# New instruction lengths for the planner of a two-problem sliding-window attention kernel

## The chip, the cores and the metric

The kernel runs on one core of a Trainium2 chip. The metric is device time in microseconds (us): medians of several executions, each with a 95% interval where two kernels are compared. All timed runs quoted here were fast, at a granted TensorE clock of 0.997 to 1.0.

## The reference

Two independent problems A and B of the same shape are computed and their outputs are put side by side:

```python
B, S, D = 1, 2048, 1024;  H = 32; Dh = 32; W = 256
qkv = (x @ wqkv)                        # 2048x1024 @ 1024x3072, bf16
scores = q @ k^T * Dh**-0.5             # causal, and only the last 256 keys
p = softmax(where(mask, scores, -1e9))
out = (p @ v) @ wo                      # 1024x1024
```

With blocks of 128 queries and 128 keys, the window leaves 45 blocks of scores per head instead of 256. Four heads are handled together (a "group"), so there are 16 groups, 8 per problem.

## The kernel before

The kernel runs in 180 **rounds**. A round computes the scores of four blocks for four heads into the one score buffer in PSUM (four times the size of a `pp` bank, see below), and ScalarE takes the exp of them in one instruction of 2048 columns. In 128 places between rounds TensorE adds up PV and the row sums (PV) of an earlier pair of query blocks. What is left of the round is filled with **projection chains**: eight 512-column steps (or sixteen of 256) that accumulate one output tile in one of two PSUM banks named `pp`. At its end a chain is copied to SBUF by a **cast**, on ScalarE or on VectorE, and the bank comes free.

A Python planner fixes this order when the program is built, with a small clock for each of three engines:

```python
NS_MM = 216.0
NS_ROW = 420.0        # scores of a round
NS_PV = 52.0          # one PV block of 128 columns
ACT_EXP = 1800.0
COST = {"act": 590.0, "dve": 670.0, "or": 560.0, "rinv": 930.0, "mult": 900.0,
        "edge": 620.0}

class _Clock:
    def chain(self):                      # a chain takes the bank that comes free next
        self.pe = max(self.pe, self.banks.pop(0))

    def evacuate(self, engines):          # who casts this chain?
        best = min(engines, key=lambda e: max(getattr(self, e), self.pe) + COST[e])
        end = max(getattr(self, best), self.pe + 150.0) + COST[best]
        setattr(self, best, end)
        self.banks.append(end)
        return best
```

`act` and `dve` are the times at which the planner believes ScalarE and VectorE to be done; `pe` is where TensorE is. The exp advances `act`, an edge add (`both`, the sum of two partly masked blocks that PV needs for its row sums) advances `dve` by `edge`. Norms come in two parts, a reciprocal (`rinv`) and two shuffles with a multiply (`mult`). These, and the ORs that gather a range check of q and k (`or`), first wait in a list called `side`:

```python
def run_side():
    cost, f, last = side.pop(0)
    f()                                   # puts the instruction into VectorE's queue
    clock.dve = max(clock.dve, clock.pe) + cost
    ...
def emit(now, budget):                    # after every projection step:
    ...
            if side and (clock.dve < clock.pe + 100.0 or len(side) > 8):
                run_side()
# in a round, after the scores:
        clock.act = max(clock.act, clock.pe) + ACT_EXP
        clock.exp = clock.act
# in the main loop: how many projection steps does the round get, and the end of the range check
    whole[0] = not (due and due[0][0] <= now)     # True: a round without PV
    ...
    emit(now, level(now) - fixed[now])            # fixed = NS_ROW + NS_PV * PV blocks
    if now >= sealed and len(certify) == 2:
        while side:
            run_side()                            # all that waits is flushed
        certify.pop(0)(top)                       # the check is read on VectorE
```

## Time and profile before

Time: 609.83 us median of 3 runs (609.81 to 610.95); with the runs beside the changed kernel, 609.85 us median of 6.

| | busy us | share |
|---|---|---|
| TensorE | 593.6 | 98% |
| VectorE | 468.4 | 77% |
| ScalarE | 441.1 | 73% |
| casts on ScalarE / VectorE | 191 / 66 | |
| rounds, first to last scores | 539.9 | |

### The profile page before, as it was taken

The page shows a single profiled execution, that of the slowest core. Times are in us where ns is not written, and L with a number is a line of the kernel's source. Part 1 is how long each engine was busy: PE and PEld are TensorE (multiplying, and loading weights), DVE is VectorE, ACT ScalarE, POOL GpSimd, SP SyncE. Part 2 cuts the span into 40 slices and gives each one's busy share as a digit, 9 for nine tenths or more (in the row PEclk, how much of TensorE's full clock was granted, in tenths as well). Part 3 has the DMA queues.
Part 4 walks back from the last instruction along what each step waited for, and adds up shares of the span by engine and source line. Part 5 has one row for each costly group of instructions (what it writes and reads, how often), then busy time and mean ns, then how long its engine had stood idle before and what let it go on. Part 6 is the DMA issues. An engine that isn't in the chain of part 4 may idle for free.

```text
span 607.6 us, 28768 instructions
## 1 busy us (share of the span) xinstructions
PE 593.6 (98%) x12786; PEld 344.3 (57%) x12838; DVE 468.4 (77%) x1199; ACT 441.1 (73%) x376; POOL 326.3 (54%) x630
## 2 busy tenths in 40 slices
PE   8999999999999999999999999999999999999996
PEld 6555466656655756564556756655455665545443
DVE  1677889898898898897888887898888887897200
ACT  3778887788888887877778877777776777785332
POOL 0565666665666666556555565555555655554000
PEclk9999999999999999999999999999999999999999
DMA  9833110111015501442111100112021040113222
GB/s 234 182 92 89 37 38 3 38 38 39 3 38 90 114 14 30 82 101 77 38 37 38 38 4 8 33 37 81 2 68 34 4 106 21 55 58 120 72 79 64
DMA packets 86802, 35.47 MB, mean 58 GB/s; under 512 B 65552, under 2 KB 86160, under 8 KB 86672
## 3 DMA queue, kind: packets, MB, share of 16 engines
q1 hardware_dynamic: 85632, 33.31, 22.2%
q8 instruction: 102, 1.67, 1.2%
q10 hardware_dynamic: 1040, 0.26, 0.2%
q14 instruction: 28, 0.23, 0.1%
HBM read 17.83 MB, written 8.39 MB: 43 GB/s over the span
## 4 chain that ended last, share of the span: by engine, by line
PE 96%; ACT 2%; issue 1%; DMA 1%; ACTq 0%
PE pp L176 44%; PE pp L172 28%; PE acc L513 13%; PE st L451 10%; ACT pt L459 1%; DMA oT<-in_A_x_dram 1%; PE acc L582 0%; PE pp L568 0%; ACT kT L190 0%; ACT vt L190 0%; PE st L582 0%; ACT osb L190 0%; PE pp L805 0%; ACTq L190 0%
## 5 line engine op out<-in xcount | busy, mean ns | idle before, releaser
L459 ACT ACTIVATE pt<-st 128x2048 bf16<-128x2048 f32 x180 | 338.0, 1878 | 91.6 <-PE st L451 73.5
L471 POOL TENSOR_SCALAR_AFFINE_SELECT pt<-pt 128x512 bf16<-128x512 bf16 x224 | 154.5, 690 | 145.7 <-ACT pt L459 143.1
L467 POOL TENSOR_SCALAR_AFFINE_SELECT pt<-pt 128x512 bf16<-128x512 bf16 x256 | 179.2, 701 | 85.8 <-ACT pt L459 85.8
L524 DVE RECIPROCAL rinv<-acc 128x128 f32<-128x128 f32 x128 | 122.0, 953 | 57.0 <-PE acc L513 56.4
L176 PE MATMUL pp<-xT,wqk 128*32 128x512 bf16 x2712 | 163.1, 379 | 0.0
L481 DVE TENSOR_TENSOR both<-pt 128x512 bf16<-128x512 bf16 x224 | 137.1, 651 | 0.0
L176 PEld LDWEIGHTS <-wqk 128*32 128x32 bf16 x2712 | 69.3, 97 | 54.2 <-issue 0.4
L172 PE MATMUL pp<-xT,wqk 128*128 128x512 bf16 (+1 forms) x323 | 76.7, 369 | 4.1 <-issue 2.4
L176 PE MATMUL pp<-wv,xT 128*32 128x256 bf16 x2436 | 75.9, 273 | 0.0
L451 PE MATMUL st<-qT,kT 32*128 32x384 bf16 (+2 forms) x1488 | 71.5, 269 | 0.1
L176 PEld LDWEIGHTS <-xT 128*32 128x32 bf16 x2436 | 63.8, 97 | 6.2
L529 DVE STREAM_SHUFFLE wide<-rinv 128x128 f32<-128x128 f32 x256 | 64.6, 298 | 0.0
L513 PE MATMUL acc<-pt,vt 128*32 128x128 bf16 (+1 forms) x2160 | 63.3, 239 | 0.0
L172 PE MATMUL pp<-wo_sb,oT 128*128 128x512 bf16 (+1 forms) x269 | 59.3, 373 | 1.3 <-issue 0.9
L451 PEld LDWEIGHTS <-kT 32*128 32x128 bf16 x1488 | 22.2, 92 | 64.5 <-issue 63.3
L190 ACT CAST osb<-pp 128x512 bf16<-128x512 f32 (+1 forms) x52 | 30.0, 577 | 39.1 <-PE pp L172 24.4
L531 DVE TENSOR_TENSOR oT<-acc,wide 128x256 bf16<-128x256 f32 x128 | 54.3, 425 | 4.4
L176 PE MATMUL pp<-wo_sb,oT 128*32 128x512 bf16 x952 | 55.6, 379 | 0.0
L172 PEld LDWEIGHTS <-wqk 128*128 128x128 bf16 x362 | 33.4, 98 | 37.0 <-issue 6.8
L172 PE MATMUL pp<-wv,xT 128*128 128x256 bf16 x415 | 50.9, 273 | 1.4 <-ACT kT L190 0.6
L513 PEld LDWEIGHTS <-vt 128*32 128x32 bf16 x2160 | 35.9, 96 | 26.4 <-issue 24.1
L172 PEld LDWEIGHTS <-xT 128*128 128x128 bf16 x415 | 38.9, 98 | 12.0 <-issue 6.1
(46 smaller groups left out, 386.5 us busy)
## 6 DMA issues: line engine op xcount, KB each, us to landing
out_dram<-osb SPq DMA_DIRECT2D x63, 128.0 KB, 1.8
wqk<-in_B_wqkv_dram SPq DMA_DIRECT2D x32, 128.0 KB, 2.5
wqk<-in_A_wqkv_dram SPq DMA_DIRECT2D x24, 128.0 KB, 2.7
wo_sb<-in_A_wo_dram SPq DMA_DIRECT2D x16, 128.0 KB, 2.2
wv<-in_B_wqkv_dram SPq DMA_DIRECT2D x16, 128.0 KB, 2.8
wo_sb<-in_B_wo_dram SPq DMA_DIRECT2D x16, 128.0 KB, 2.4
oT<-in_A_x_dram SPq DMA_DIRECT2D x4, 256.0 KB, 5.4
wv<-in_A_wqkv_dram SPq DMA_DIRECT2D x2, 512.0 KB, 5.9
```

Of the source, the lines that this page charges most:

```text
L172: nc.tensor.matmul(out[:, lo:hi], lhsT=lhsT, rhs=rhs, start=start, stop=stop, skip_group_check=True)
L176: nc.tensor.matmul(out[c:c + 32, lo:hi], lhsT=lhsT[:, c:c + 32], rhs=rhs, start=start, stop=stop, tile_position=(0, c), skip_group_check=True)
L190: nc.scalar.copy(out=out, in_=in_)
L451: nc.tensor.matmul(st[:, r, a:b, :], lhsT=kT[32 * r:32 * r + 32, j * P:(j + 1) * P], rhs=qT[32 * r:32 * r + 32, q * P:(q + b - a) * P], st ...
L459: nc.scalar.activation(out=pt[:, :, :n, :].rearrange("p r a q -> p r (a q)"), in_=st[:, :, :n, :].rearrange("p r a q -> p r (a q)"), func= ...
L467: nc.gpsimd.affine_select(out=blk, in_=blk, pattern=[[0, 4], [1, P]], compare_op=ALU.is_ge, fill=0.0, base=0, channel_multiplier=-1)
L471: nc.gpsimd.affine_select(out=blk, in_=blk, pattern=[[0, 4], [-1, P]], compare_op=ALU.is_gt, fill=0.0, base=0, channel_multiplier=1)
L481: nc.vector.tensor_tensor(out=both[:, :, h, :], in0=pts[s0][:, :, a0, :], in1=pts[s1][:, :, a1, :], op=ALU.add)
L513: nc.tensor.matmul(acc[32 * r:32 * r + 32, o:o + w_], lhsT=lhsT, rhs=src[:, r, :, :], start=(x == 0), stop=(x == len(moves) - 1), tile_pos ...
L524: nc.vector.reciprocal(out=rinv[:], in_=acc[:, 2 * P:3 * P])
L529: nc.vector.stream_shuffle(out=wide[:, h * P:(h + 1) * P], in_=rinv[:], mask=[16 * h] * 32)
L531: nc.vector.tensor_tensor(out=oTs[(pi, k)][:, t, (p % 2) * 256:(p % 2 + 1) * 256], in0=acc[:, 0:256], in1=wide[:], op=ALU.mult)
```

## The change

The new lengths of ScalarE's and VectorE's work lie 1 to 8% above the mean durations that the trace of the kernel before shows (the exp 1878 ns, an edge add 651, an OR 528, a reciprocal 953, two shuffles and a multiply 1021 added up). No instruction, buffer or load changes.

```diff
-NS_ROW = 420.0
-NS_PV = 52.0
+NS_ROW = 440.0
+NS_PV = 55.0
-ACT_EXP = 1800.0
-COST = {"act": 590.0, "dve": 670.0, "or": 560.0, "rinv": 930.0, "mult": 900.0,
-        "edge": 620.0}
+ACT_EXP = 1900.0
+COST = {"act": 610.0, "dve": 700.0, "or": 570.0, "rinv": 970.0, "mult": 1080.0,
+        "edge": 680.0}
-        clock.act = max(clock.act, clock.pe) + ACT_EXP
+        clock.act = max(clock.act, clock.pe + 100.0) + ACT_EXP
```

## The prediction

> **What bounds the kernel now.** I read the page's engine totals and slices first, then the chain that ended last, then the table of who waited for whom, then the timeline of one round. First the page:
>
> ```profile
> span 607.6 us, 28768 instructions
> ...
> PE 593.6 (98%) x12786; PEld 344.3 (57%) x12838; DVE 468.4 (77%) x1199; ACT 441.1 (73%) x376; POOL 326.3 (54%) x630
> ...
> PE   8999999999999999999999999999999999999996
> ...
> PEclk9999999999999999999999999999999999999999
> ...
> PE 96%; ACT 2%; issue 1%; DMA 1%; ACTq 0%
> ```
>
> TensorE is busy in every slice at full granted clock, and 96% of the chain that ended last lies on it. A busy share alone is not proof, as matmul ends are modelled, so I ask what TensorE waited for. These are the lines of the wait table in which a matmul waited for ScalarE or VectorE (line, releaser, us in total, times, longest), and, in the second block, three for the other engines:
>
> ```profile
> PE pp L172 <- ACT vt L190: 1.0, 2, 0.5
> PE pp L172 <- ACT kT L190: 0.6, 2, 0.4
> PE pp L172 <- DVE oT L531: 0.3, 2, 0.2
> ```
>
> ```profile
> POOL pt L471 <- ACT pt L459: 143.1, 110, 2.0
> ...
> ACT pt L459 <- PE st L451: 73.5, 113, 1.3
> ...
> DVE rinv L524 <- PE acc L513: 56.4, 64, 3.3
> ```
>
> In the whole run matmuls waited 1.0 + 0.6 + 0.3 = 1.9 us for another compute engine; the other engines wait for TensorE (or for the exp that TensorE feeds) for tens of microseconds. The planner's orders are about such waits, so 1.9 us, 0.3% of the span, is roughly all that a better order can win.
>
> One round ("session") of the timeline (start us, us, engine, line, what), TensorE's rows only:
>
> ```profile
> 299.84 0.40 PE L451 MATMUL st<-qT,kT 32*128 32x128 bf16 x8
> ...
> 300.17 0.51 PE L513 MATMUL acc<-pt,vt 128*32 128x128 bf16 x16
> ...
> 300.51 0.28 PE L513 MATMUL acc<-pt,ones 128*32 128x128 bf16 x8
> 300.62 0.28 PE L513 MATMUL acc<-both,ones 128*32 128x128 bf16 x8
> ...
> 300.73 1.15 PE L176 MATMUL pp<-wv,xT 128*32 128x256 bf16 x36
> ...
> 301.71 1.25 PE L176 MATMUL pp<-xT,wqk 128*32 128x512 bf16 x20
> ...
> 302.90 0.40 PE L451 MATMUL st<-qT,kT 32*128 32x384 bf16 x8
> ```
>
> Start to start: scores 0.33 us, PV and row sums 0.56 us (ten blocks of 0.056), then projections until 302.90. The projections are 36 quarter-width matmuls of 256 columns (9 steps of 0.108) and 20 of 512 columns (5 steps of 0.216), 2.05 us of work in 2.17 us; the last 0.12 us goes to the change of array tiling back to scores. There is no gap into which an earlier cast would let TensorE move.
>
> **The fixed sum.** Projections: 2 problems x 2048 x 1024 x 4096 multiply-adds / (128 x 128 x 512) = 2048 matmuls x 0.216 = 442.4 us. 180 rounds of scores with both tiling changes, 0.33 + 0.11 = 0.44: 79.2 us. PV: 112 groups of 10 blocks and 16 (the first pair of each head group) of 6 make 1216 blocks x 0.056 = 68.1 us. Together 589.7 us. Before the first scores (13.83 us) there are 8.6 us that are not projection work (16 + 8 full-matmul equivalents, 5.2 us, are), and after the last matmul (602.2 us) 5.4 us of cast and store. 589.7 + 8.6 + 5.4 = 603.7 of 607.6 us; the other 3.9 are the 1.9 us of waits and my rounding. The change touches none of the three terms.
>
> **The Trainium skill.** "TensorEngine Tiling (Array Packing)", Key Properties, says that changing the tiling mode drains TensorE; the trace agrees, with the 0.11 to 0.12 us lost on each side of the scores, and the count of changes (two per round) comes from the round structure, not from the constants. "TensorE: Matmul & The Clock Gate", Back-to-back issue gap, gives 518 cycles at 2.4 GHz, 216 ns, for an isolated 512-column matmul; its sustained 131 ns does not appear here, a step takes 216. "Perfetto Trace Analysis", Optimizing Scalar/DVE Operations, says that a profiled latency overstates engine-busy time because the write acknowledgement overlaps the next instruction. The trace agrees: two edge adds in a row start at 142.87 and end 1.19 us later, 0.595 each, while the table's mean for one is 0.651.
>
> **The change part by part.** No instruction is added or removed, no buffer, no load. Only numbers change in the clock by which the planner chooses (a) whether a PSUM cast goes to ScalarE or VectorE, (b) after which projection step a norm or a range-check OR enters VectorE's queue, (c) how many projection steps a round gets.
>
> (c) A round with a full PV costs the planner 420 + 10 x 52 = 940 ns before and 440 + 10 x 55 = 990 after; TensorE really spends 0.44 + 0.56 = 1.00 us, so the new figure is right. But the budget is level minus this figure, and the level is the mean of the same figures plus the available work over the rounds to come, so the shift cancels but for 30 ns between rounds with and without PV. Against steps of 108 and 216 ns this moves a step across a round border now and then. The ceiling of 3300 ns is not what sets the length: rounds take some 2.85 us in the first half and 3.05 to 3.15 later. TensorE's sum is unchanged: 0 us.
>
> (a) and (b) Here are the groups that the costs describe (busy us, mean ns):
>
> ```profile
> L459 ACT ACTIVATE pt<-st 128x2048 bf16<-128x2048 f32 x180 | 338.0, 1878 | 91.6 <-PE st L451 73.5
> ...
> L524 DVE RECIPROCAL rinv<-acc 128x128 f32<-128x128 f32 x128 | 122.0, 953 | 57.0 <-PE acc L513 56.4
> ...
> L481 DVE TENSOR_TENSOR both<-pt 128x512 bf16<-128x512 bf16 x224 | 137.1, 651 | 0.0
> ```
>
> The exp takes 1878 ns: 1800 was short, 1900 is right. The reciprocal takes 953 (930, now 970). The norm's second part is two shuffles of 298 and a multiply of 425: 1021 added up, but 140.65 to 141.61 = 0.96 us on the timeline, since the shuffles overlap; 900 was short by 60, 1080 is long by 120. An edge add at 0.595 to 0.651 is nearer to 620 than to 680. What the planner thinks VectorE has to do: before, 128 x (930 + 900) + 224 x 620 + 128 x 560 + 66 casts x 670 = 489 us; after, with the same casts, 128 x 2050 + 224 x 680 + 128 x 570 + 66 x 700 = 534 us, against 468 measured. The rounds last 540 us (14 to 554), so the planner will now take VectorE for full, which it is not. ScalarE: 180 x 1800 + 191 x 590 = 437 us before, 180 x 1900 + 191 x 610 = 459 after (441 measured), and each exp now starts 100 ns later in the model. Both engines look later, VectorE by 45 us and ScalarE by 22 plus 18 of the start delays. The choice of a cast compares the two backlogs, so the split shifts by little: today 191 on ScalarE and 66 on VectorE; I expect 45 to 80 on VectorE, without being sure of the sign. Norms and ORs come later in VectorE's queue, which lets casts in ahead of them.
>
> For the time: the waits for casts (1.6 us) may go to 0.5 or to 3; the waits for norms (0.3 us on matmuls, under 1 us with weight loads) may grow by a microsecond. Sum: -1.5 to +2, centre 0.
>
> **The rivals.** (1) The better exp and cast lengths remove the remaining waits: 1.9 us, giving 608.0. For it: the exp was 80 ns short in the model and the worst waits (0.5 us each) follow a ScalarE cast queued behind an exp. Against: five-odd events in 180 rounds are no systematic error, and other rounds can get such events in their place. (2) Too many casts go to ScalarE: in the short rounds (2.85 us) an exp of 1.88 and 1.65 casts of 0.58 would need 2.84 us, ScalarE would be full, the next scores would wait for their only buffer, and rounds would stretch. If every cast went there, perhaps 0.1 us in half of the rounds, 9 us: 619. Against: only a quarter of the casts can still move, and ScalarE idles 91.6 us ahead of its exps. (3) Norms pushed back hold the two PV accumulators: VectorE is 77% busy and nearly 90% in the middle, so a norm of 1.96 us that enters late could hold PV for a few tenths; in a tenth of 128 groups that is 3 to 4 us: 613. Against: a norm is forced into the queue before the PV after next, and VectorE waits 56 us for PV today.
>
> **Range and chances.** Centre 609.6 us: the median before, less a small share of rival 1. Range 607.5 to 613: below by the whole 1.9 us and noise (the three runs span 1.1 us), above by rival 3. 2% is 12 us: faster by so much is out of reach, as waits to be removed total 1.9 us; slower needs rival 2 in full.
>
> **What would show it.** Right: TensorE 98% busy, 180 rounds with the same 0.33 + 0.56 us, matmul waits for ScalarE and VectorE between 0.5 and 4 us, casts on VectorE between 45 and 80, the last PV near 565 us and the last matmul near 602. Wrong: exp lines that wait for casts while scores then wait for exp (rival 2), or PV weight loads waiting for the norm's multiply by microseconds (rival 3), or rounds that bunch so that projection work runs out before the end.

## More of the kernel before

Below is one round without PV, as it is wanted: the timeline of the kernel before (start us, us, engine, line, operation, result<-inputs, count, idle before and its releaser). Other rows are left out.

```profile
287.36 0.40 PE L451 MATMUL st<-qT,kT 32*128 32x256 bf16 x8
...
287.81 1.88 ACT L459 ACTIVATE pt<-st 128x2048 bf16<-128x2048 f32 x1 [1.22 <-PE st L451]
...
287.92 2.54 PE L172 MATMUL pp<-wo_sb,oT 128*128 128x512 bf16 x11 [0.16 <-issue]
...
288.85 0.68 DVE L192 CAST kT<-pp 128x512 bf16<-128x512 f32 x1
...
289.89 0.59 ACT L190 CAST osb<-pp 128x512 bf16<-128x512 f32 x1 [0.20 <-PE pp L172]
...
290.39 0.40 PE L451 MATMUL st<-qT,kT 32*128 32x128 bf16 x8
```

A chain ends one step after the scores. Its cast (`kT`) is on VectorE at 288.85, while ScalarE is in the exp until 289.69. The other bank takes the next chain; by the time that chain is full the first bank is free, and TensorE runs through: 3.03 us from scores to scores.

## The result, and the profile after

The changed kernel takes 613.23 us (median of 6, 612.66 to 613.67) against 609.85: ratio 1.0052, 95% interval 1.0039 to 1.0065. A ratio here compares mean times of fast runs, so it is not quite the ratio of the medians. The difference is within 2%, but clear of noise, and the time lies just above the predicted range (613.0).

The page of the changed kernel, engine totals:

```profile
span 611.5 us, 28734 instructions
...
PE 594.7 (97%) x12765; PEld 344.6 (56%) x12817; DVE 447.4 (73%) x1171; ACT 454.5 (74%) x404; POOL 329.3 (54%) x630
```

TensorE's work is the same. VectorE lost 21 us and ScalarE gained 13: 28 casts moved, 219 on ScalarE and 38 on VectorE now. The matmuls' waits after the change:

```profile
PE pp L172 <- ACT kT L190: 1.4, 4, 0.4
...
PE pp L172 <- ACT vt L190: 0.7, 2, 0.4
PE pp L176 <- DVE unsafe_i L806: 0.7, 1, 0.7
PE pp L172 <- ACT qT L190: 0.4, 1, 0.4
PE pp L176 <- ACT kT L190: 0.4, 1, 0.4
...
PE acc L513 <- DVE both L481: 0.2, 1, 0.2
```

Waits for ScalarE's casts went from four (1.6 us) to eight (2.9 us), and two new waits for VectorE appeared. The last matmul ends 3.42 us later (605.59 against 602.17). Laying the starts of the 180 score groups of both traces side by side splits these 3.42 us:

| stretch | before | after | difference |
|---|---|---|---|
| start to first scores | 13.83 | 13.70 | -0.13 |
| first to last scores | 539.92 | 542.27 | +2.35 |
| last scores to last PV | 11.28 | 12.49 | +1.21 |
| last PV to last matmul | 37.14 | 37.13 | -0.01 |

**The 2.35 us.** Most of the rounds that differ do so by a step of 0.108 or 0.216 in one direction, and a later one by the same in the other: a step moved across a border. Run e4 below has the same `NS_ROW` and `NS_PV` as the changed kernel, and the weight loads in its trace stand in the same order, so comparing with e4 takes these shifts out. Seven rounds of the changed kernel are longer than in e4, by 0.23, 0.25, 0.28, 0.57, 0.15, 0.56 and 0.55 (at 89, 155, 187, 287, 306, 363 and 373 us; 2.59 together). In five of them (89, 155, 287, 363, 373) the planner, run alone, sends a cast of that round to ScalarE that goes to VectorE in e4. One round is shorter by 0.85 (at 28 us, where e4 waits for a load), and no other differs by more than 0.04. The moved steps, e4 against the kernel before without that load, come to -0.25, with the shorter waits at 141 and 242 us among them. Here is the round shown before, in the changed kernel:

```profile
287.63 0.40 PE L451 MATMUL st<-qT,kT 32*128 32x256 bf16 x8
...
288.08 1.88 ACT L459 ACTIVATE pt<-st 128x2048 bf16<-128x2048 f32 x1 [0.75 <-PE st L451]
...
288.19 1.89 PE L172 MATMUL pp<-wo_sb,oT 128*128 128x512 bf16 x8 [0.16 <-issue]
...
289.31 0.41 DVE L184 TENSOR_TENSOR top<-top,kT 128x256 int32<-128x256 int32 x1
289.75 0.42 DVE L184 TENSOR_TENSOR top<-top,qT 128x256 int32<-128x256 int32 x1
289.86 0.58 ACT L190 CAST kT<-pp 128x512 bf16<-128x512 f32 x1
...
290.49 0.81 PE L172 MATMUL pp<-wo_sb,oT 128*128 128x512 bf16 x3 [0.41 <-ACT kT L190]
...
291.23 0.40 PE L451 MATMUL st<-qT,kT 32*128 32x128 bf16 x8
```

The same chain ends one step after the scores, but its cast now goes to ScalarE, where an exp of 1.88 us has just begun. It starts at 289.86 instead of 288.85. The next chain is full before that cast is done, both banks are taken, and TensorE stands still until 290.49. Meanwhile VectorE does two ORs that nobody waits for. The record shows 0.41 us of waiting; the round is 0.57 us longer.

**The 1.21 us.** It lies where the range check is closed. The end of the changed kernel:

```profile
556.87 0.42 DVE L184 TENSOR_TENSOR top<-top,kT 128x256 int32<-128x256 int32 x1
557.33 0.29 DVE L798 TENSOR_SCALAR top<-top 128x256 int32<-128x256 int32 x1
...
558.46 1.59 DVE L481 TENSOR_TENSOR both<-pt 128x512 bf16<-128x512 bf16 x2
...
560.11 0.24 PE L513 MATMUL acc<-both,ones 128*32 128x128 bf16 x4 [0.18 <-DVE both L481]
...
560.84 0.08 DVE L806 TENSOR_SCALAR unsafe_i<-pp 1x1 int32<-1x1 f32 x1
...
561.00 3.64 PE L176 MATMUL pp<-wo_sb,oT 128*32 128x512 bf16 x64 [0.65 <-DVE unsafe_i L806]
```

From 553.05 to 557.29 VectorE does seven ORs in a row, of which the last is shown. They had waited in `side`, because the planner believed VectorE busy, and are flushed when the check is sealed. So the edge adds come late for PV, and the tiny read that frees a `pp` bank (`unsafe_i`) comes later still. In the kernel before, one OR was left at that point, and the same read came 0.2 us after its matmul:

```profile
556.99 0.16 PE L805 MATMUL pp<-okp,ones 128*1 128x1 f32 x1
...
557.22 0.14 DVE L806 TENSOR_SCALAR unsafe_i<-pp 1x1 int32<-1x1 f32 x1 [1.15 <-PE pp L805]
```

### The profile page after: what moved, and what is told of

It reads as the page before. It is cut to its first block, busy times and chain, and to the rows that moved or that the text cites. A ratio compares the mean times of both kernels' runs of the same rounds, so it can differ in the third digit from the quotient of the medians.

```text
span 611.5 us, 28734 instructions
## 1 busy us (share of the span) xinstructions
PE 594.7 (97%) x12765; PEld 344.6 (56%) x12817; DVE 447.4 (73%) x1171; ACT 454.5 (74%) x404; POOL 329.3 (54%) x630
## 4 chain that ended last, share of the span: by engine, by line
PE 93%; ACT 3%; issue 1%; DMA 1%; DVE 1%; SPq 0%; ACTq 0%; DVEq 0%
PE pp L176 42%; PE pp L172 28%; PE acc L513 13%; PE st L451 10%; ACT pt L459 2%; DMA oT<-in_A_x_dram 1%; ACT kT L190 0%; DVE rinv L524 0%; PE acc L582 0%; ACT vt L190 0%; ACT osb L190 0%; DVE top L184 0%; DVE qT L192 0%; DVE both L481 0%; PE pp L568 0%
## 5 line engine op out<-in xcount | busy, mean ns | idle before, releaser
L459 ACT ACTIVATE pt<-st 128x2048 bf16<-128x2048 f32 x180 | 338.0, 1878 | 84.5 <-PE st L451 63.6
L481 DVE TENSOR_TENSOR both<-pt 128x512 bf16<-128x512 bf16 x224 | 132.4, 631 | 0.0
```

What stands on the lines that cost most here:

```text
L459: nc.scalar.activation(out=pt[:, :, :n, :].rearrange("p r a q -> p r (a q)"), in_=st[:, :, :n, :].rearrange("p r a q -> p r (a q)"), func= ...
L481: nc.vector.tensor_tensor(out=both[:, :, h, :], in0=pts[s0][:, :, a0, :], in1=pts[s1][:, :, a1, :], op=ALU.add)
```

## The experiments

My theory after these readings: the new VectorE lengths are too long, since they count whole durations of instructions that overlap. The planner then sees VectorE late, sends a few badly placed casts to ScalarE, and lets ORs pile up. The rivals: the longer exp or the TensorE lengths do it; ScalarE has room, and only the order of norms matters; or the plan is a lottery, in which any disturbance moves the time by a few us.

Each kernel was timed over five rounds (e13 six runs). Counts of early ScalarE casts and of flushed operations in the expectations come from running the planner alone, without a chip; the counts of casts on VectorE agree with the traces.

### e5: the changed kernel with a short list

```diff
-            if side and (clock.dve < clock.pe + 100.0 or len(side) > 8):
+            if side and (clock.dve < clock.pe + 100.0 or len(side) > 2):
```

> The changed kernel, but an OR or norm part is forced out as soon as more than 2 wait instead of more than 8, so about 1 range-check OR instead of 7 is left when the checks are sealed; casts as in the changed kernel (37 on VectorE by the plan, 38 there). Theory (two separate losses: about 2.2 us of waits for PSUM banks behind ScalarE casts, about 1.2 us at the end from the pile of ORs): 612.0 us, the waits of the third-last PV group for an edge add and for the safety decision gone, the eight waits for ScalarE casts still there. Rival (the plan is simply a lottery, any disturbance gives a random result): anything from 608 to 615, no particular place. Rival (the casts alone cost 3.4 us): 613.2.

Measured: 612.16 us against 609.44 before (1.0046, 1.0033 to 1.0060). In its trace the stretch from last scores to last PV is 11.28 us again, the same as before the change, and both VectorE waits are gone. The rounds kept their eight waits for ScalarE casts; the round of the one at 74 us got 0.36 us longer, that of the one at 190 us 0.28 shorter. By the trace the gain over the changed kernel should be 1.0 us; the medians against the kernel before differ by 2.72 in place of 3.38, 0.66 less, from runs in different rounds. What makes up the rest is open. So the end loss is the pile of ORs, and it is the smaller part.

### e6: the kernel before with casts moved to ScalarE

```diff
-        best = min(engines, key=lambda e: max(getattr(self, e), self.pe) + COST[e])
+        best = min(engines, key=lambda e: max(getattr(self, e), self.pe) + COST[e]
+                                          + {"act": 0.0, "dve": 200.0}[e])
```

> The kernel before with all its lengths, but VectorE gets a handicap of 200 ns in the choice of an engine for a cast, so 36 of 257 casts are on VectorE (66 before, 38 in the changed kernel), and no pile of ORs at the end. Theory (a cast moved to ScalarE waits behind an exp and holds a PSUM bank): matmul waits for ScalarE casts rise from 4 to about 8, and the time by about 2.2 us to 612.0. Rival (ScalarE has room, 91.6 us idle ahead of its exps, so moved casts are free and the loss is all in the order of norms and ORs): 609.8.

Measured: 611.43 us (1.0031, 1.0017 to 1.0045), near the expected time, but with five recorded waits for ScalarE casts instead of about eight. The order of TensorE's instructions is identical with that of the kernel before, so rounds compare one to one: five rounds without PV, at 297, 306, 363, 372 and 381 us, got longer by 0.21, 0.56, 0.16, 0.14 and 0.20, no other by more than 0.06. Only one of these shows as a recorded wait for a cast; in the others there is a gap ahead of a weight load, which the profile puts down to "issue", as at 363 us:

```profile
366.45 0.31 PEld L172 LDWEIGHTS <-wqk 128*128 128x128 bf16 x2 [0.27 <-issue]
```

The rounds account for 1.35 of the 2.0 us; the rest is not explained (the first scores came 0.7 us later in the profiled run, but that start lies anywhere from 13.6 to 14.8 us in the traces of these kernels). Casts on ScalarE are not free, but how many of them is a poor measure, as the next run shows.

### e7: the changed kernel with casts given back

The same edit with -100.0 for `dve`, in the changed kernel.

> The changed kernel with all its lengths, but VectorE is favoured by 100 ns in the choice for a cast, so 73 casts are on VectorE, and the pile of ORs at the end stays (the plan leaves as many as in the changed kernel). Theory: waits for ScalarE casts go back to 4 or fewer, the end loss of 1.2 us stays: 611.0 us. Rival (casts are not it, the later norms and ORs are): 613.2.

A miss: 613.54 us (1.0067, 1.0053 to 1.0081), no better than the changed kernel. VectorE has 73 casts again, yet 23 of the 35 that came back lie after 556 us, where no exp runs and ScalarE is idle anyway. The waits at 160, 229, 246, 292, 368 and 378 us are all still there; at 292 us, for one, the planner expects VectorE to end the cast 284 ns after ScalarE, so a favour of 100 does not turn the choice. The rounds lose a new 0.55 us at 40 us, where PV waits for a norm, and win 0.28 at 188 us; the end loss is 0.91. The share of casts is not the cause; their places are.

### e8 and e9: six single casts

```diff
+        self.count += 1
         best = min(engines, key=lambda e: max(getattr(self, e), self.pe) + COST[e])
+        if self.count in (61, 74, 115, 147, 151, 155):
+            best = "dve"
```

> The changed kernel with all its lengths, but six single casts, counted in the planner's order (61, 74, 115, 147, 151, 155), are sent to VectorE by force. The first five are those at which the changed kernel's trace shows a new wait for a ScalarE cast (at 158, 190, 290, 366 and 376 us); the sixth would go to ScalarE in the same position once the others are moved. The previous experiment gave 35 other casts back and none of these, and won nothing. Theory (what costs is not the share of casts on ScalarE but these few, emitted within three steps of the scores of a round without PV, when an exp has just begun): those five waits vanish, the waits at 74, 227 and 245 us and the 1.2 us at the end stay, 610.6 us, about 2.5 below the changed kernel. Rival (VectorE is really late there, so PE waits for VectorE in place of ScalarE): 613, with waits for VectorE casts at those times.

> The same six casts by force and, as in e5, at most 2 waiting norm parts and ORs. Theory (the two losses add up and are all of it): 609.5 us, the same as the kernel before within 0.5 us. Rival (a third cause, for example the changed round budgets, stays): 611 or more.

Measured: e8 611.83 us (1.0037, 1.0023 to 1.0050), e9 610.73 (1.0015, 1.0002 to 1.0029), both against 609.75. Both came out about 1.2 us above their theory (610.6 and 609.5). Forcing the six moved two other casts back to ScalarE. Four of the five waits vanished in e8: the rounds at 155, 287, 363 and 373 us are shorter than in the changed kernel by 0.57, 0.46, 0.41 and 0.40, and no other round moved. The fifth did not go, as the rival had it for this place: TensorE waits for VectorE instead. The line in e8's trace (its lines are shifted by four):

```profile
189.97 0.40 PE L180 MATMUL pp<-xT,wqk 128*32 128x512 bf16 x4 [0.37 <-DVE kT L196]
```

So four casts out of 257 carry 1.84 us of the loss in the traces; in the medians e8 is 1.3 us nearer to the kernel before than the changed kernel is. In e9 the end loss is gone (11.28 us), but its rounds are still 0.9 us slower than before. Against e4, which has the same order of TensorE's work, e9 keeps 0.36 at 72 us (the wait that the short list makes longer), 0.28 at 90, 0.25 at 188 (the wait for VectorE) and 0.11 to 0.15 in four more rounds, and one round (156 us) is 0.32 shorter. The two losses are thus most of the loss and not all of it; what is left sits in these small waits, and not in the budgets.

### e2 and e1: the VectorE lengths alone, and all but them

e2 is the kernel before with `or`, `rinv`, `mult` and `edge` new; e1 is the changed kernel with these four old.

> The kernel before with only the four VectorE lengths changed (or 570, rinv 970, mult 1080, edge 680). The plan puts 23 casts on VectorE and leaves 6 to 7 operations piled up at the end. Theory (too long VectorE lengths cause both losses): at least as slow as the changed kernel, 613 to 615. Rival (the exp or TensorE lengths, or the cast lengths, cause it): 609.8 to 611.

> The changed kernel with only the four VectorE lengths taken back (or 560, rinv 930, mult 900, edge 620); exp, its start, TensorE and cast lengths stay new. The plan has 79 casts on VectorE, three ScalarE casts early in a round without PV (74, 227, 245 us) where the kernel before has four, and a pile of ORs at the end as before it is sealed (6 flushed, 8 in the changed kernel, 2 in the kernel before). Theory (the VectorE lengths are the cause of the casts): 609 to 610.3 us, depending on whether the pile costs anything. Rival (exp or TensorE lengths cause it): 612 to 613.

Measured: e2 613.38 us against 609.44 (1.0066, 1.0052 to 1.0079); e1 610.39 against 609.75 (1.0012, 0.9998 to 1.0026). The four VectorE lengths alone make a loss as large as the whole change, and without them the rest of the change costs nothing that is clear of noise. e2 loses 3.68 us in its rounds (23 casts on VectorE, eight rounds longer by 0.15 to 0.63) and nothing at the end, so its end pile was harmless. By the planner eight operations are flushed in the changed kernel, e7 and e8, where the end costs 0.91 to 1.21 us, and six or seven in e1, e2, e3 and e14, where it costs 0 to 0.20. The end loss of the changed kernel thus does not come from the four lengths alone; which of the others it needs was not tested. In e1 the places at 287, 363 and 373 us have no wait; one PV at 41 us waits 0.49 us for the multiply of a norm, and the end costs 0.19.

### e3 and e4: the rivals alone

e3 changes only the exp (1900, and 100 ns later) in the kernel before, e4 only `NS_ROW` and `NS_PV`.

> The kernel before with only the exp made longer and later (1900, 100 ns after the scores). The plan has 76 casts on VectorE, the same four early ScalarE casts as the kernel before (74, 143, 227, 244 us), and 6 operations flushed at the end instead of 2. Theory (the exp figure is right and pushes casts away from ScalarE, so it costs nothing): 609.4 to 610.0 us, the same as before, with at most 0.3 us of waiting at the end. Rival (a later exp is part of the loss): 611 or more.

> The kernel before with only the round and PV lengths of TensorE changed (440, 55). They move projection steps across round borders as in the changed kernel; the plan has 65 casts on VectorE and three early ScalarE casts (74, 227, 245 us; the one at 143 us goes). Theory (the budgets are not the cause): 609.3 to 609.8 us. Rival (moved round borders create the coincidences): 611 or more.

Measured against 609.71: e3 610.52 us (1.0012, 0.9998 to 1.0026), e4 609.75 (0.9999, 0.9986 to 1.0013). e3 came out above its expectation, not clear of noise: its trace has the four old ScalarE waits, the PV wait of 0.49 us at 41 us that e1 has too, and 0.4 us of waiting for a first load. e4 moves the steps across round borders as the changed kernel does (the same rounds shift by 0.21 and back) and costs nothing by its median; its profiled run waited 0.67 us for a first load. Four kernels with other plans than before (e1, e3, e4, e13) stayed within noise of it, so the plan does not look like a lottery either.

### e14: lengths from spacing

In these traces VectorE's instructions overlap, so what one occupies is the distance from its start to that of the next, back to back. From the timeline of the kernel before, means of such distances: reciprocal 0.975 us (0.995 when its own shuffle follows, 0.872 when something else does), shuffle 0.269 (0.206 to the second shuffle, 0.332 to the multiply that reads both), multiply 0.343, so `mult` is 2 x 0.269 + 0.343 = 0.88; an edge add 0.58; an OR 0.49; a cast 0.60. By this measure the old norm (930 + 900 ns, against 1855) was right, and the new one is 195 ns long.

```diff
-COST = {"act": 610.0, "dve": 700.0, "or": 570.0, "rinv": 970.0, "mult": 1080.0,
-        "edge": 680.0}
+COST = {"act": 610.0, "dve": 700.0, "or": 490.0, "rinv": 980.0, "mult": 880.0,
+        "edge": 580.0}
```

> The changed kernel with the four VectorE lengths taken from the start-to-start spacing of back-to-back instructions in the trace of before instead of from the sum of their durations: or 490, rinv 980, mult 880, edge 580. Theory (durations overlap, so adding them overstates VectorE's load; spacings don't): 87 casts on VectorE, two early ScalarE casts left (227 and 245 us), 608.5 to 609.5 us, faster than before by up to 1 us if the end pile (6 flushed) costs nothing. Rival (VectorE now gets more than it can do and norms come late): PV waits for norms, 611 or more.

Measured: 608.54 us against 609.75 (0.9985, 0.9971 to 0.9998). This beats both kernels, the one before by a margin barely clear of noise. Two waits for ScalarE casts are left in the wait table of the eight, and its rounds take 538.76 us against 539.92:

```profile
PE pp L172 <- ACT kT L190: 0.4, 1, 0.4
PE pp L172 <- ACT vt L190: 0.3, 1, 0.3
```

### e13 and e15: a rule for the bad places

```diff
+        if whole[0] and clock.pe - clock.scored < 700.0:   # scored: pe just after the scores
+            engines = ("dve",)
         if clock.evacuate(engines) == "act":
```

e13 is this rule in the kernel before; e15 adds it and the short list to e14.

> The kernel before with all its lengths and one rule more: a cast that falls within 700 ns of model time after the scores of a round without PV goes to VectorE whatever the clocks say. Theory (these casts are the whole of the waits that the kernel before has left): the four waits of the trace vanish, 4 x 0.57 = 2.3 us less, 607.3 us. Rival (VectorE is behind at these places, so TensorE waits for its cast instead): 608.5 to 610 with waits for VectorE casts.

> VectorE lengths by spacing (or 490, rinv 980, mult 880, edge 580) with the changed kernel's other lengths, the rule for early casts, and at most 2 waiting norm parts and ORs. Theory: 608.5 less the two waits left in e14 (0.57 + 0.47) and 0.2 us at the end, 607.3 us, below both kernels. Rival (as for the rule): 608.5.

Both missed, as the rivals said: e13 609.45 us (0.9998, 0.9986 to 1.0011), e15 608.93 (0.9990, 0.9977 to 1.0004), against 609.71. Of the four waits of the kernel before, the one at 74 us vanished; the other three turned into waits for VectorE. The lines of e13:

```profile
143.21 0.38 PE L173 MATMUL pp<-xT,wqk 128*128 128x512 bf16 x1 [0.33 <-DVE vt L195]
...
226.40 0.60 PE L173 MATMUL pp<-wv,xT 128*128 128x256 bf16 x4 [0.21 <-DVE kT L195]
...
244.25 0.71 PE L173 MATMUL pp<-wv,xT 128*128 128x256 bf16 x5 [0.68 <-DVE vt L195]
```

At these three places VectorE really is behind, so the rule wins little: the rounds at 141 and 224 us got 0.16 and 0.18 shorter, the one at 242 us 0.19 longer, and the one at 72 us, whose wait vanished, 0.35 shorter. That is 0.5 us in the trace and not clear of noise in the medians. In e15 the rule leaves waits for VectorE of 0.66 and 0.19 us, and its rounds take 539.06 us, no less than e14's.

## Why the prediction was wrong

**The bound and the fixed sum: right.** TensorE's work did not change, 180 rounds with the same pieces. The ceiling of the gain, 1.9 us, was not contradicted (the best version found gains 1.2 us), but its working is loose: the wait table also has 1.3 us before the first matmul, which the prediction left out and the planner does not order, and recorded waits understate what they cost (below).

**Budgets (c): right.** Steps moved across borders and back, and e4, which changes these lengths alone, is at 0.9999.

**VectorE's load (a, b): the reading was right in the main, the step after it failed.** The prediction said that the planner would take VectorE for full at 534 us against 468 measured. (One reading was off: the 0.96 us for a norm's second part runs from the first start to the last end. By spacing it is 0.88, so 900 was not short, and 1080 is long by 200 and not by 120.) It then argued that both clocks shift by similar amounts, "so the split shifts by little", 45 to 80 casts on VectorE. The trace has 38. The two shifts do not cancel. The planner, run alone, shows how late it believes each engine to be behind TensorE at the start of a round: for VectorE, means over 30 rounds went up by 0.25 to 0.74 us (most in rounds 30 to 89, from about 1.0 to 1.7), for ScalarE by 0.07 to 0.20, about what the exp's new length and start add within one round. At the cast of the round at 287 us VectorE was 1024 ns behind TensorE before and 1978 after, ScalarE 1584 and 1784. The choice turned.

So the step that failed is "the split shifts by little", and with it the centre of 0 for "the waits for casts (1.6 us) may go to 0.5 or to 3". Recorded waits for ScalarE casts rose to 2.9 us, inside that span, but the rounds lost 2.35 us, more than the 1.3 us that the recorded waits grew by: such a wait can cost more than is recorded (0.57 for 0.41 in the round shown), and some show only ahead of weight loads. The sum's upper end, +2, held neither this nor the end loss below; measured is +3.4. That 613.23 lies so near the upper end of the range is chance, as that end came from rival 3.

**Norms and ORs: a term was missing.** "Norms and ORs come later in VectorE's queue, which lets casts in ahead of them" reads as a help, and only the waits for norms were allowed to grow. The ORs that come later pile up to seven, and flushing them costs 1.21 us at the end. No term of the sum held this flush at the seal.

**The rivals.** Rival 2 (too many casts to ScalarE) was the right mechanism in another form: it was put as ScalarE filling up, with scores waiting for exp. That did not happen; ScalarE is 74% busy. What happened is two waiting banks behind one exp, at a handful of places, e6 and e8. Rival 1 (better exp and cast lengths remove waits) fell with e3, where all four waits stay, and e1, which has both and is no faster than before. Rival 3 (norms hold PV) shows as one wait of 0.49 us in e1, e3 and e7; in the changed kernel no matmul waits for a norm.

What stays open: which of the four lengths weighs most was not run one by one. By the planner's sums, the added load, 128 x 180 ns for `mult` and 224 x 60 ns for `edge`, is 23 and 13 us, against 5 and 1 for the other two.

## What to carry to other kernels

A planner's clock for an engine should advance by what an instruction occupies, the spacing from start to start of back-to-back instructions, and not by the duration that the trace prints; here too long lengths kept the believed lag of a nearly full engine too large for many rounds. That spacings are better is shown by one kernel (e14), against the kernel before by a margin barely clear of noise. When an instruction can go to one of two engines, what counts is what it queues behind and who waits for its buffer, at the few places where both buffers are taken, and not how many go where. A list of deferred work that is flushed at one point is a wait to be counted at that point.

## What the Trainium skill lacked or had wrong

- "Perfetto Trace Analysis", Optimizing Scalar/DVE Operations, gives about 60 ns of overhead for VectorE on SBUF and about 125 ns on PSUM, with a profiled latency of about twice that, as the other half overlaps with the next instruction; from these figures one would expect, as an estimate, overlaps of about 60 and 125 ns. Here the overlap, from back-to-back pairs in the trace of the kernel before, is nearly one size: 76 ns for edge adds (659 long, 583 apart) and 78 for ORs, both in SBUF, and 78 to 83 for casts, multiplies and reciprocals, which read PSUM (a multiply 424 and 342).
- "VectorE: DVE Perf Modes", The DRAIN you can't avoid, says that the next instruction starts only when the pipe is empty, and in the same paragraph that one that is not held starts earlier. Here it is mostly the second: a shuffle of 298 ns is followed by the next shuffle after 206. The multiply, which reads the shuffles' results, starts 332 ns after the second of them, so after its end.
- No page says how far recorded matmul waits fall short of what they cost: 0.41 us recorded where the round is 0.57 us longer, and rounds 0.14 to 0.21 us longer (e6) with no wait for a cast recorded at all.
